# Retention and a cosine-gated MLP on one core: the first block by pairs of heads, and loads and weight differences in another order

## The chip, the cores and the metric

The kernel runs on one core of a Trainium2 chip. A core has five engines, each with a queue of its own: TensorE (PE; its weight loads are shown apart as PEld), VectorE (DVE), ScalarE (ACT), GpSimd (POOL) and SyncE (SP), which here only issues DMAs. All DMAs of a core run on the same 16 DMA engines. The metric is the time of one execution in microseconds (us) of device time, with all inputs in HBM at the start and the output in HBM at the end.

## The reference

```python
# q, k, v: [8 batches, 8 heads, 576 positions, 64], float32
scores = q @ k.transpose / sqrt(64)
gamma  = 1 - 2 ** (-5 - head)
Dmat   = gamma ** (i - j) for i >= j, else 0
attn   = (scores * Dmat) @ v
x      = attn, as [8 * 576 tokens, 8 * 64 = 512]
h      = x @ w_in          # [512, 2048]
out    = (h * cos(h)) @ w_out      # [2048, 512]
```

There is no softmax, so the retention can be computed block by block with a carried state, the running sum of k (transposed) times v.

## The kernel before, in words

**Retention.** The 4608 tokens are cut into 18 blocks `j` of 256. The decay is split: q is scaled by gamma to the power of its position (`gq`), k by gamma to the negative power (`gkp` for blocks 0 and 1, `gkc` for the rest), so that within a chunk the scores only need a mask of ones and zeros. The steps of a block are:

- `load(j)`: q, k and v from HBM by DMAs on SP. Blocks 0 and 1 put two neighbouring tokens into one partition (512 bytes in a run), and later blocks do so only for q.
- `scaled` (line 174): q or k times its decay, cast to bf16, one call for each of two token rows `y`. `prep(j)` issues the four calls of a block on GpSimd.
- `round_v` (line 185): v cast to bf16.
- `transpose_pe` (blocks 0 and 1, line 225) or `turned` (line 210): transposes on TensorE into a PSUM bank, which are then copied to `qkT` (lines 230 and 216).
- `scores` (lines 264 and 302): the matmuls of k and q by chunk, and the mask multiplication `masked` on VectorE, which writes `ret` (lines 282 and 311).
- `sums_of` (lines 352 and 335): the state matmuls of k and v. It returns `add`, which adds up the state `s_all` (lines 367 to 384), and that returns `rounded`, the copy to bf16 `sb` (line 394).
- `outputs`: `out_own` (line 420), `ret` times v; `out_carried` (line 447), the carried state times q; then the copy of PSUM `ov` to `xT` (lines 466, 853 and 499).

**MLP.** Two blocks make a window `n` of 512 tokens; there are nine. `mm1` (line 490) multiplies `w_in` by `xT` into PSUM `h`, four or two 128-column tiles at a time, ScalarE computes the cosine (line 503) and VectorE multiplies (line 506) into `gT`. The second product is plain in window 0 (line 991); from window 1 on it is done with seven instead of eight quarter products (`mm2_seven`, line 610), for which differences and sums of quarters of `w_out` (`w_sums`, line 529) and of `gT` (`g_sum`, line 549) are formed, mostly on VectorE. `w_sums` runs once, in window 0: (5, e0), (6, e0), (4, e0) and (7, e0), each for e0 = 0 and 4.

**Order.** The schedule is manual: each engine executes its instructions in the order in which the program issues them, and waits only for data and for buffers to come free. The opening (lines 760 to 871) is written out by hand. The queues around it are:

- SP: `load(0)`, `load(1)` with v behind k's landing, then `load_next` for blocks 2, 3 and 4. The first has a gate: its first DMA waits until the fourth `w_in` load has landed. That of block 3 waits for the third `w_out` load.
- GpSimd: position tables, `ident` and masks, the first `w_in` load, k of block 1, the other three `w_in` loads, half of v of block 1, `w_out` loads 0 and 4, load 8 (which waits for the landing of load 0, by `after`), k of block 2, `w_out` load 12, a half of q of block 2, then v of block 2 and `prep(3)`. Behind these stands `prep(4)`, which is issued in window 1. The weight loads convert float32 to bf16 on the way.
- `warm(n, tag)` puts n matmuls of zeros with 512 columns into a PSUM bank: fillers for TensorE.

In window 0 the matmuls of line 991 are issued in a loop with a counter `done` (0 to 63), and a list `todo` says which other step is issued at which count, lowest first: scaling, turning and scoring of blocks 2 and 3 and the weight differences. At equal count the order of the list holds. The results in PSUM (`o`, two parts in bank "m", one each in "n" and "st") are copied out by ScalarE and VectorE in turn (line 1001), and the first `mm1` of window 1 writes bank "m" again.

PSUM banks are named by tags: "a", "b" and "m" hold 4 KB per partition, "n" and "st" 2 KB. Each has one buffer, so a new tile in a bank waits until all readers of the old one are done.

## Time and profile before

| | |
|---|---|
| median of 3 runs | 296.82 us (296.63 to 296.84) |
| profiled execution | 296.85 us, its span 295.1 us |
| TensorE / VectorE / ScalarE / GpSimd busy | 284.5 / 215.2 / 170.5 / 143.4 us |
| first `h` matmul of window 0 | at 15.52 us |
| first `o` matmul of window 0 | at 31.69 us |
| first `h` matmul of window 1 | at 49.44 us |
| granted TensorE clock | 1.00 |

The rows of the time line read: start, duration, engine, source line, operation, output and inputs by the program's names, form, count; in brackets the idle time of the engine before it and what ended it. Rows of equal instructions close together are merged: the duration is then that of the whole row. Starts of instructions on one engine can lie closer together than their durations, since they overlap at the ends. Busy matmuls are modelled and overlap too. "SPq" and "POOL ... DMA_DIRECT2D" are the issues of DMAs, and "to landing" is the time from issue until the last of the data is there.

### The profile page before, as it was taken

What the parts mean: (1) busy time and instruction counts of PE and PEld (TensorE: products, weight loads), DVE (VectorE), ACT (ScalarE), POOL (GpSimd) and SP (SyncE); (2) the same over time, 40 slices, a digit from 0 to 9 for tenths busy, and PEclk for the clock granted to TensorE, in tenths of its full rate; (3) what the DMA queues carried; (4) which work ended last, traced back from release to release, by engine and by line L of the source; (5) the groups of instructions that cost most, each with busy time, mean ns of one, the idle gap of its engine ahead of it and who ended that gap; (6) DMA issues with size and microseconds to landing.
All of it is one profiled execution on the core that took longest, in us unless ns stands there. A gap on an engine that the chain in (4) does not pass through costs nothing.

```text
span 295.1 us, 10506 instructions
## 1 busy us (share of the span) xinstructions
PE 284.5 (96%) x4367; PEld 196.3 (67%) x4388; DVE 215.2 (73%) x300; ACT 170.5 (58%) x200; POOL 143.4 (49%) x163
## 2 busy tenths in 40 slices
PE   7899999999999999999999999999999999999994
PEld 2578545878864687468745884588458845884584
DVE  5756767758857887698769866986698669745943
ACT  3676317476558844767476737674768466535620
POOL 8621439970585995349434942495249014102400
PEclk9999999999999999999999999999999999999999
DMA  7999999999989857833873396429201130112013
GB/s 222 289 206 224 227 251 233 260 231 221 227 189 232 218 134 173 201 71 98 213 189 77 78 225 176 100 52 257 58 0 40 38 73 0 40 47 62 2 36 107
DMA packets 103981, 42.62 MB, mean 144 GB/s; under 512 B 68480, under 2 KB 103424, under 8 KB 103936
## 3 DMA queue, kind: packets, MB, share of 16 engines
q1 hardware_dynamic: 99184, 37.37, 51.8%
q0 software_dynamic: 4224, 4.19, 8.7%
q8 instruction: 36, 0.59, 0.9%
q10 hardware_dynamic: 528, 0.39, 0.4%
q14 instruction: 9, 0.07, 0.1%
HBM read 36.70 MB, written 9.44 MB: 156 GB/s over the span
## 4 chain that ended last, share of the span: by engine, by line
PE 83%; DVE 5%; ACT 3%; DMA 3%; POOL 2%; SPq 1%; issue 1%; ACTq 0%; DVEq 0%
PE h L490 41%; PE o L610 32%; PE ov L420 3%; PE tr L210 2%; POOL qks L174 2%; DMA fq<-in_q_dram 2%; PE ov L447 1%; PE sc L302 1%; DMA fk<-in_k_dram 1%; DVE gT L506 1%; PE st L335 1%; ACT cosh L503 1%; SPq L153 1%; DVE qks L174 1%; DVE ret L282 1%
## 5 line engine op out<-in xcount | busy, mean ns | idle before, releaser
L490 PE MATMUL h<-xT,w_in_sb 128*128 128x512 bf16 (+1 forms) x689 | 126.8, 340 | 1.3 <-DVE qkT L216 0.4
L506 DVE TENSOR_TENSOR gT<-h,cosh 128x1024 bf16<-128x1024 f32 x72 | 87.7, 1222 | 33.5 <-ACT cosh L503 33.1
L490 PEld LDWEIGHTS <-w_in_sb 128*128 128x128 bf16 x704 | 68.1, 98 | 55.2 <-issue 1.1
L503 ACT ACTIVATE cosh<-h,half_pi 128x1024 f32<-128x1024 f32 x72 | 79.9, 1115 | 40.5 <-PE h L490 40.5
L549 POOL TENSOR_TENSOR gs<-gT 128x512 bf16<-128x512 bf16 x28 | 35.8, 1277 | 100.4 <-DVE gT L506 100.4
L610 PEld LDWEIGHTS <-gs 128*128 128x128 bf16 x528 | 49.7, 98 | 5.9
L610 PEld LDWEIGHTS <-gT 128*128 128x128 bf16 x384 | 36.6, 98 | 6.1
L636 DVE TENSOR_TENSOR ot<-ot,o 128x512 f32<-128x512 f32 x35 | 23.2, 683 | 22.4 <-ACT ot L640 14.2
L174 POOL TENSOR_TENSOR qks<-fk,gkc 128x512 bf16<-128x512 f32 x32 | 37.1, 1178 | 2.8 <-DMA fk<-in_k_dram 2.8
L174 POOL TENSOR_TENSOR qks<-fq,gq 128x512 bf16<-128x512 f32 x31 | 34.7, 1137 | 7.5 <-DMA fq<-in_q_dram 7.5
L216 ACT COPY qkT<-tr 128x1024 bf16<-128x1024 bf16 x29 | 27.7, 1022 | 6.4 <-PE tr L210 6.4
L394 ACT CAST sb<-s_all 128x768 bf16<-128x768 f32 (+2 forms) x18 | 16.3, 904 | 25.6 <-DVE s_all L384 21.6
L610 PE MATMUL o<-w_out_sb,gs 128*128 128x256 bf16 (+1 forms) x264 | 30.6, 269 | 0.1
L610 PE MATMUL o<-w_out_sb,gT 128*128 128x256 bf16 x256 | 30.6, 273 | 0.0
L610 PE MATMUL o<-ws,gs 128*128 128x256 bf16 (+1 forms) x264 | 30.5, 269 | 0.0
L640 ACT COPY ot<-o 128x512 f32<-128x512 f32 x33 | 19.3, 584 | 16.0 <-PE o L610 16.0
L311 DVE TENSOR_TENSOR ret<-sc,mask_c 128x512 bf16<-128x512 f32 x32 | 20.7, 685 | 7.3 <-PE sc L302 7.3
L185 POOL CAST vb<-fv 128x512 bf16<-128x512 f32 x31 | 19.3, 646 | 4.8 <-DMA fv<-in_v_dram 4.8
L466 ACT CAST xT<-ov 128x1024 bf16<-128x1024 f32 x16 | 16.2, 1012 | 9.4 <-PE ov L447 9.2
L384 DVE TENSOR_TENSOR s_all<-st,s_all 128x256 f32<-128x256 f32 x49 | 20.7, 422 | 1.2
L549 DVE TENSOR_TENSOR gs<-gT 128x512 bf16<-128x512 bf16 (+1 forms) x25 | 16.7, 668 | 0.5
L610 PE MATMUL o<-ws,gT 128*128 128x256 bf16 x128 | 15.3, 273 | 0.0
(73 smaller groups left out, 207.0 us busy)
## 6 DMA issues: line engine op xcount, KB each, us to landing
out_dram<-ot SPq DMA_DIRECT2D x68, 128.0 KB, 2.6
fk<-in_k_dram SPq DMA_DIRECT2D x28, 256.0 KB, 4.9
fv<-in_v_dram SPq DMA_DIRECT2D x28, 256.0 KB, 4.8
fq<-in_q_dram SPq DMA_DIRECT2D x12, 512.0 KB, 5.1
w_in_sb<-in_moe_w_in_dram POOLq DMA_DIRECT2D x4, 512.0 KB, 8.0
w_out_sb<-in_moe_w_out_dram POOLq DMA_DIRECT2D x4, 512.0 KB, 8.3
fq<-in_q_dram SPq DMA_DIRECT2D x4, 384.0 KB, 5.1
fk<-in_k_dram SPq DMA_DIRECT2D x2, 512.0 KB, 4.9
```

What stands on the lines that cost most here:

```text
L174: return eng.tensor_tensor(out=dst.rearrange("p b a d -> p a b d"), in0=src.rearrange("p (a b) d -> p a b d", a=2), in1=by.rearrange("p (a ...
L185: runs[y](vb[:, y], f[:, :, y, :] if j < NP_B else f[:, y])
L216: evacs[r](tiles["qkT", j][:, :, :, :, r * HP : r * HP + HP], pss[r])
L311: nc.vector.tensor_tensor(out=ret[:, he].rearrange("p b y i -> p (b y) i"), in0=ps[he].rearrange("p b y i -> p (b y) i"), in1=mask_c.unsqu ...
L384: nc.vector.tensor_tensor(out=s32[:, u], in0=ps[c.half][:, c.y], in1=s32[:, u - 1] if u else tiles["run"], op=ALU.add,)
L490: nc.tensor.matmul(ps[:, j, :], lhsT=w_in_sb[:, dg, (et + j) * P : (et + j + 1) * P], rhs=xT[:, dg, c0 : c0 + w], start=(dg == 0), stop=(d ...
L503: nc.scalar.activation(cosh, ps, ACTF.Sin, bias=half_pi, scale=1.0)
L506: nc.vector.tensor_mul(gT[:, et : et + m, c0 : c0 + w], ps, cosh)
L549: i = eng.tensor_tensor(out=tiles["gs", n, x][:, e : e + step], in0=a[:, e : e + step], in1=b[:, e : e + step], op=op_,)
L610: nc.tensor.matmul(dst[i], lhsT=lhs[:, e, j * P : (j + 1) * P], rhs=rhs[:, e, c0:c1], start=(fresh and e == 0 and (i == 0 or len(parts) > 2)),
L636: return lambda: nc.vector.tensor_tensor(out=out_, in0=in0, in1=in1, op=ALU.add)
L640: held.append(lambda ps=tiles["all", x]: nc.scalar.copy(t, ps))
```

## The change

1. **Loads of block 0.** q and k of block 0 are loaded in two halves `g` of the heads (heads 0, 1, 4, 5 and then 2, 3, 6, 7), each by two DMAs, in the order k, q, k, q. Of the first halves one DMA each goes on ScalarE's queue, all others on SP. v follows as before.
2. **Block 0 by pairs of heads.** Scaling, transposes, copies, scores and masks are issued by halves: `scaled_heads`, `turned_heads`, `scores` with a range of head pairs. The copies of the transposes are all on ScalarE, and the masks come in two lots of 512 columns a head group instead of one of 1024. v is rounded half on GpSimd. The fillers are 8, 1, 1, 2 and 2 instead of 11, 2, 3, 2 and 2.
3. **Outputs of block 0 first.** `out_own(0)` now comes before the first transposes of block 1, and the copy to `xT` right behind `out_carried(0)` and ahead of the rest of block 1; q of block 1 is scaled, turned and copied row by row, one of the copies on ScalarE.
4. **Gates.** Block 2's loads wait for the third `w_in` load instead of the fourth, `w_out` load 8 no longer waits, and block 3's loads wait for the second `w_out` load instead of the third.
5. **Window 0's list.** Scores and state of block 2 are issued at 38 and 39 instead of 40 and 41; the weight differences (6, 0), (4, 0), (7, 0) come behind them instead of at 34 to 36; q of block 3 is scaled on VectorE at 40, its k on GpSimd; then the differences (6, 4), (4, 4), (7, 4) at 41 to 43 instead of 51 to 53.

Branches that no call used are removed from `scores` and `prep`.

```diff
+    def load_heads(name, g):
+        src = {"q": q, "k": k}[name]
+        if ("f" + name, 0) not in tiles:
+            tiles["f" + name, 0] = ld.tile([P, H, 2, D], F32, tag="f" + name, name=f"f{name}")
+        f = tiles["f" + name, 0]
+        for he in range(2):
+            h0 = he * HG + 2 * g
+            (nc.scalar if he and not g else nc.sync).dma_start(
+                f[:, h0 : h0 + 2].rearrange("p h r d -> p h (r d)"),
+                src[0, h0 : h0 + 2, :BK, :].rearrange("h (p r) d -> p h (r d)", r=2),
+            )
+
+    def scaled_heads(eng, name, g):
...
+        for y in range(2):
+            eng.tensor_tensor(
+                out=dst[:, y],
+                in0=f[:, y],
+                in1=by[:, y, 2 * g : 2 * g + 2].unsqueeze(3).to_broadcast([P, 2, 2, D]),
+                op=ALU.mult,
+            )
+
+    def turned_heads(name, g, bank, evac=nc.scalar.copy):
...
+        ps = psum.tile([P, 2, 2, P], BF16, tag=bank, name="tr")
+        for y in range(2):
+            for u in range(2):
+                nc.tensor.transpose(
+                    ps[:, y, u, :],
+                    tiles["qks", 0][:, m, y, 2 * g + u].rearrange("s a d -> s (a d)"),
+                    ident,
+                )
+        evac(tiles["qkT", 0][:, m, :, 2 * g : 2 * g + 2], ps)
+
-    def prep(j):
-        for name in "kq" if j < NP_B else "qk":
+    def prep(j, eng_q=nc.gpsimd):
+        for name in "qk":
             for y in range(2):
-                scaled(nc.gpsimd, j, name, y)
+                scaled(eng_q if name == "q" else nc.gpsimd, j, name, y)
...
-    def scores(j, banks):
+    def scores(j, banks, g0=0, g1=HG):
...
-    load(0, "kqv")
+    for g in range(2):
+        for name in "kq":
+            load_heads(name, g)
+    load(0, "v")
     k1 = load(1, "k")
...
-    warm(11, "n")
+    warm(8, "b")
...
-    scaled(nc.vector, 0, "k", 0)
-    scaled(nc.vector, 0, "k", 1)
-    transpose_pe(0, "k", "n", act, (0,))
-    transpose_pe(0, "k", "st", act, (1,))
-    scaled(nc.vector, 0, "q", 0)
-    scaled(nc.vector, 0, "q", 1)
-    transpose_pe(0, "q", "a", act, (0,))
-    transpose_pe(0, "q", "b", vec, (1,))
+    scaled_heads(nc.vector, "k", 0)
+    turned_heads("k", 0, "n")
+    scaled_heads(nc.vector, "q", 0)
+    warm(1, "b")
+    turned_heads("q", 0, "st")
+    scaled_heads(nc.vector, "k", 1)
+    warm(1, "b")
+    turned_heads("k", 1, "m")
+    scaled_heads(nc.vector, "q", 1)
+    masks = scores(0, "ab", 0, 2)
+    turned_heads("q", 1, "n")
+    for masked in masks:
+        masked()
     w_dma = [load_w_in(0)]
-    round_v(0, (act, act))
     warm(2, "m")
-    for masked in scores(0, "ab"):
+    masks = scores(0, "ab", 2, HG)
+    round_v(0, (nc.gpsimd.tensor_copy, act))
+    for masked in masks:
         masked()
+    warm(2, "m")
     sums_of(0, "st")()()
     scaled(nc.gpsimd, 1, "k", 0)
-    warm(3, "m")
-    transpose_pe(1, "k", "n", act, (0,))
     scaled(nc.gpsimd, 1, "k", 1)
     w_dma += [load_w_in(e) for e in (512, 1024, 1536)]
-    load_next(names="kqv", gate=w_dma[3])
+    load_next(names="kqv", gate=w_dma[2])
     ps0 = psum.tile([P, DG, BK], F32, tag="m", name="ov")
     out_own(0, ps0)
-    scaled(nc.vector, 1, "q", 0)
-    scaled(nc.vector, 1, "q", 1)
-    transpose_pe(1, "k", "st", vec, (1,))
+    transpose_pe(1, "k", "n", act, (0,))
     out_carried(0, ps0)
     act(x_of(0), ps0)
+    scaled(nc.vector, 1, "q", 0)
+    transpose_pe(1, "k", "st", vec, (1,))
+    transpose_pe(1, "q", "a", act, (0,))
+    scaled(nc.vector, 1, "q", 1)
+    transpose_pe(1, "q", "b", vec, (1,))
     nc.scalar.activation(sine, half_pi, ACTF.Sin, bias=0.0, scale=1.0)
     round_v(1, (act, nc.gpsimd.tensor_copy))
-    warm(2, "n")
-    transpose_pe(1, "q", "a", vec, (0,))
-    transpose_pe(1, "q", "b", vec, (1,))
-    warm(2, "n")
     for masked in scores(1, "ab"):
         masked()
     w_dma += [load_w_out(e) for e in (0, 4)]
     w_dma.append(load_w_out(8))
-    after(w_dma[-1], w_dma[4])
     for y in range(2):
         scaled(nc.gpsimd, 2, "k", y)
     w_dma.append(load_w_out(12))
     scaled(nc.gpsimd, 2, "q", 0)
-    load_next(names="kqv", gate=w_dma[6])
+    load_next(names="kqv", gate=w_dma[5])
     load_next()
...
-                (40, lambda: adds.append(states_and_scores(2, "a", "b"))),
-                (41, lambda: adds.pop()()()),
-                (42, lambda: prep(3)),
+                (38, lambda: adds.append(states_and_scores(2, "a", "b"))),
+                (39, lambda: adds.pop()()()),
+                (40, lambda: prep(3, nc.vector)),
...
-                    (2, 5, 0), (8, 5, 4), (34, 6, 0), (35, 4, 0), (36, 7, 0),
-                    (51, 6, 4), (52, 4, 4), (53, 7, 4),
+                    (2, 5, 0), (8, 5, 4), (39.2, 6, 0), (39.4, 4, 0), (39.6, 7, 0),
+                    (41, 6, 4), (42, 4, 4), (43, 7, 4),
```

## The prediction

> **What bounds the kernel now.** I read the page first, then the time line of single engines over the first 52 us, then the landing of single loads. All times are us from the start of the span of the one profiled execution, which took 296.85 us (295.1 of span and 1.75 around it); the median of the runs shown is 296.82. The page:
>
> ```profile
> PE 284.5 (96%) x4367; PEld 196.3 (67%) x4388; DVE 215.2 (73%) x300; ACT 170.5 (58%) x200; POOL 143.4 (49%) x163
> ...
> DMA  7999999999989857833873396429201130112013
> ```
>
> TensorE is busy 96% of the span, so only its waits can be won: those ahead of the first matmul on `w_in` (15.52) and those up to some 52 us, the only stretch that the change touches. The DMA row is full from the second slice to the eleventh. TensorE from 15:
>
> ```profile
> 15.52 1.92 PE L490 MATMUL h<-xT,w_in_sb 128*128 128x256 bf16 x16
> ...
> 19.00 1.05 PE L490 MATMUL h<-xT,w_in_sb 128*128 128x256 bf16 x8
> ...
> 20.33 1.92 PE L490 MATMUL h<-xT,w_in_sb 128*128 128x256 bf16 x16
> ```
>
> After eight of the last row's matmuls (0.11 each), at 21.21, begins the third group of `w_in` columns, 1024 to 1535. The load of these columns, the third of the four on line 742:
>
> ```profile
> L742 POOL DMA_DIRECT2D w_in_sb<-in_moe_w_in_dram x1: 747/747/747, 12.2 to 12.2; - x1
> ...
> DMA to landing us min/median/max: 8.9/8.9/8.9
> ```
>
> It lands at 21.1, 0.1 before its use. The one before it lands at 18.6 (11.4 and 7.2), 0.4 before its use at 19.00. An earlier start of TensorE soon meets a weight still on its way, and the DMA engines are full ahead of it (time by stretches, last two columns their mean share and GB/s):
>
> ```profile
> 0.00:4.00 4.00, 2.75 (x7) 1.01 (x8) 1.56 (x15) 1.91 (x4) 2.73 (x21) 1.00 0.40 117
> 4.00:8.00 4.00, 3.46 (x22) 1.47 (x21) 2.79 (x4) 1.47 (x4) 3.80 (x8) 1.00 1.15 346
> 8.00:12.00 4.00, 3.04 (x86) 1.90 (x88) 3.01 (x4) 2.98 (x6) 2.58 (x3) 1.00 1.20 286
> ```
>
> The second place is the end of window 0, VectorE and then GpSimd:
>
> ```profile
> 44.71 2.60 DVE L529 TENSOR_TENSOR ws<-w_out_sb,ws 128x1024 bf16<-128x1024 bf16 x2
> 47.24 1.53 DVE L529 TENSOR_TENSOR w_out_sb<-w_out_sb 128x1024 bf16<-128x1024 bf16 x1
> 48.69 0.69 DVE L1001 COPY ot<-o 128x512 f32<-128x512 f32 x1
> ```
>
> ```profile
> 43.28 2.04 POOL L174 TENSOR_TENSOR qks<-fq,gq 128x512 bf16<-128x512 f32 x2 [2.80 <-DMA fq<-in_q_dram]
> 45.28 2.94 POOL L174 TENSOR_TENSOR qks<-fk,gkc 128x512 bf16<-128x512 f32 x2
> 48.18 2.48 POOL L174 TENSOR_TENSOR qks<-fq,gq 128x512 bf16<-128x512 f32 x2
> ```
>
> ```profile
> 47.40 0.52 PE L210 MATMUL tr<-ident,qks 64*128 64x64 bf16 x24
> 48.27 0.29 PE L210 MATMUL tr<-ident,qks 64*128 64x64 bf16 x8 [0.35 <-POOL qks L174]
> 48.50 1.04 PE L991 MATMUL o<-w_out_sb,gT 128*128 128x512 bf16 x4
> 49.44 1.47 PE L490 MATMUL h<-xT,w_in_sb 128*128 128x256 bf16 x12
> ```
>
> Two things are to be seen. TensorE loses 0.5 at 48.27, where block 3's transposes wait for GpSimd. And the first `h` of window 1 starts at 49.44, 0.06 after VectorE's copy of `o` (48.69 and 0.69) has emptied PSUM bank "m", which this `h` takes. So VectorE's queue is a limit there too. In it the weight differences (line 529) took 1.15, 1.42 and 1.53 beside GpSimd's scalings, against 0.68 with GpSimd idle (34.18), and GpSimd's k took 1.49 each against 1.04: starts lie 1.45 apart when they alternate, 0.605 when VectorE runs alone.
>
> **The change, part by part.** First the loads of block 0. Two loads of 512 KB become eight of 128 KB, six on SP, two on ACT. Bytes and the DMA engines are the same, and the data of k was all there at 4.67 (0.80 and 3.9); half of it I put at 3.9, since at 346 GB/s the other 256 KB take 0.75. On SP the six issues at 0.43 to 0.57 take 3 us where two took 1.0, and v of block 0, then k, q and v of block 1, stand behind them; the engines are full meanwhile, so this is hidden, as long as an issue of 128 KB (0.38 us of transfer at 346 GB/s) does not cost more than it carries. If it did, block 0's four pairs would be issue-bound: bound 0 to +1.0. I take 0. On ACT two issues go ahead of the table load (0.80 and 1.28), which then ends near 3.1, ahead of the first exponential at 3.28: hidden.
>
> The chain of block 0: eight scalings of 256 columns (0.34 each by 0.60 for 512, 0.42 beside GpSimd's masks) from 4.0, when both k and the decay (3.28 and 0.23, then `kpos` until 3.87 on VectorE) are there, until 7.3 instead of 7.6. Transposes and copies follow by pairs; scores of the first two head pairs near 7.1 to 7.7, masks 4 x 0.62 in two lots, the second until 10.2 to 10.7 instead of 11.78. State matmuls 9.8 to 10.8, outputs 10.8 to 11.8 instead of 12.7. Rounding v moves half to GpSimd, free from 7.97 until k of block 1 at 9.4: hidden.
>
> Block 1's transposes now stand behind. VectorE's order is q row 0, copy of k row 1, q row 1, copy of q row 1. The copy of k waits for TensorE (12.8), so q row 1 comes at 13.3 to 13.9, its transposes at 14.0, its copy until 14.8, the scores at 14.85, the first `h` at 15.45. What the first block gained, the order of the second gives back: -0.07. Were it 0.3 earlier, the weight landing at 21.1 would take all but 0.1 of it. GpSimd's queue up to the `w_in` loads has only the half round of v put in, inside its wait; those loads land as before. Sum of the first part: -0.1 to +0.3, and I take 0.
>
> Loads of blocks 2 and 3: SP's gate goes from the fourth `w_in` load (23.6) to the third (21.1), and the third `w_out` load no longer waits for the first (GpSimd stood 8.35 us for that, in front of k of block 2). The order on the engines changes, their work does not; fq of block 2 comes earlier than 35.9 and the sums need nothing of it before 37.8. The fourth `w_out` load still follows k of block 2 on GpSimd. If k lands only at 32, behind the third `w_out` load, the fourth is issued near 34 instead of 32.03; landing took 7.1 then (39.1), so it is there by 41, and its first use is at 43.6, hidden by the `o` matmuls; past that, each us late would cost one. Nothing else waits on these in 31 to 42: 0.
>
> End of window 0, where X is the first part's shift. Scores of block 2 are issued two matmuls of 0.213 earlier, at 40.67; masks (0.61 x 2, by 1.28 for the two at 42.27) from 41.4, state adds until 43.86 instead of 44.71, so the carried outputs no longer wait for the state (0.28 won, 45.72 in the trace). VectorE is idle for 1.2 before it, having nothing else in front. After it come three weight differences, q of block 3 (two, new on VectorE), and three differences: eight operations at 0.605, until 48.70 alone, then the copy of `o` until 49.35. That is the same 49.4 as now: what VectorE is spared of GpSimd (2.4) it pays with q (1.2) and idleness (1.2). TensorE would be ready for `h` at 48.65, and waits.
>
> So the question is what GpSimd does from 43.86 to 48.70. Its k of block 3 should be over by 43.9 (data near 40.8). Next in its queue are q of block 4, whose second load was issued at 43.85 and landed 4.1 later, at 47.95. The bytes ahead of it are unchanged, so I keep 48.0, with 0.5 either way. At 48.05 seven of the eight are over or running; GpSimd takes the turn, the last difference comes 0.85 later (1.45 less 0.605), the copy ends at 50.25, `h` starts at 50.3: +0.86. Block 3's scores, which now wait 0.16 for a copy on ACT (51.03), then don't. Sum +0.7.
>
> That price is 0.85 a turn by the rows. [...]
>
> **The rivals.**
> No turn: q of block 4 lands after 48.1, or GpSimd comes too late. Then `h` starts at 49.40 and the ACT wait is gone: -0.2, 296.6. For it: 0.1 of margin only. Against: nothing delays that load.
> Two or more turns: block 3's gate is earlier and the DMA share fell to 0.59 in 40 to 41 and 0.84 in 44 to 45; closed, these gaps bring q of block 4 up to 0.6 earlier, to 47.4, where two differences are left: +0.7 and 0.85, 298.4.
> Faster, the other side: two queues fill the engines sooner. The first 4 us moved 117 GB/s, and if the full rate came 0.85 earlier, k of block 1 and all weights would land that much earlier, and block 1's chain with them; with the first `h` at 14.9 and no turn lost the sum is -0.5 and -0.2, 296.1. It decides once the third `w_in` load lands before 20.6.
> The array's clock: the fillers fall from 20 to 14, and seven that stood between 10 and 14.6 become two before 9.9. In the trace fillers started 0.43 apart until 5.9 and 0.22 apart at 7.9, with the granted clock at 1.00 throughout. If TensorE met `h` at the slow pace, 16 matmuls would cost 0.11 more each, +1.75, 298.6, or with issue-bound loads +1.0. [...]
>
> **How the numbers follow.** 0.2% is 0.6 us, about what a measurement of this kernel can tell from no change. One turn, my forecast: 0.38, of which 0.05 inside the 0.6. No turn: 0.20. Faster, with ways that I don't see: 0.20. Two or more turns: 0.14. Clock or issue-bound loads: 0.08. So faster 0.20, same 0.25, slower 0.55. The time is 296.82 and 0.7: 297.5. The range reaches down past the faster case by its own margin, 295.9, and up to two turns with the first part at +0.3 and half a turn more, 299.2. The forecast case alone spans 297.3 to 297.9.
>
> **What would show it.** Right: the third `w_in` load lands near 21.1 and TensorE's third group begins with it; the first `h` of window 1 starts on the heels of VectorE's copy of `o` at 50 or later, with a TensorE gap above 1 ahead of it; the last of the eight VectorE operations takes over 1.1 beside GpSimd's q of block 4; block 3's transposes no longer wait. Wrong: an `h` there before 49, eight operations of 0.68 throughout, or weights that land before 20.6.

## The result: slower, by twelve microseconds, and not by the same amount each time

The changed kernel took 309.23 us (median of 4, 304.81 to 311.14) against 296.83 for the kernel before: a ratio of 1.0324, 95% interval 1.0231 to 1.0417. Forecast were 297.5 and, as the range, 295.9 to 299.2. In a later group of runs the same kernel took 299.08, 306.55, 307.99 and 309.36. The ratios below leave out executions of over 1.5% above the quickest of their kernel, so for kernels that vary the whole spread of times is given too.

Two profiled executions of the changed kernel, one of 310.42 us and one of 299.08, are read beside each other. Times are from the start of the span. The page of the long one, with the lines that answer to those shown of before, and the granted clock:

```profile
PE 290.7 (94%) x4382; PEld 198.5 (64%) x4382; DVE 217.7 (71%) x306; ACT 171.5 (56%) x201; POOL 142.5 (46%) x162
...
PEclk9958999879999999999999999999999999999999
DMA  7999999997933894782488157906600140022013
```

TensorE is busy 6.2 us longer for the same work (290.7 against 284.5). Of the 40 slices of the clock, of 7.7 us each, the third is at 5 (half), the fourth and the eighth at 8 and the ninth at 7; before, all were whole. The DMA row is full from the second slice to the ninth, then thin in the twelfth and thirteenth. In the rows of the changed kernel the same steps have other line numbers: the scaling is L214 (174 before), rounding v L225 (185), `mm1` L520 (490), the weight differences L559 (529), the second product L1027 (991), the copy of `o` L1037 (1001).

| | before | changed, 310.42 | changed, 299.08 |
|---|---|---|---|
| q of block 1: scaling on VectorE can start | 10.71 (landed) | 16.50 | 11.80 |
| third `w_in` load lands | 21.10 | 22.91 | 21.81 |
| first `h` of window 0 | 15.52 | 20.40 | 15.57 |
| first `o` of window 0 | 31.69 | 38.64 | 32.35 |
| fourth `w_out` load lands | 39.09 | 45.05 | 44.69 |
| list of eight VectorE operations begins | | 50.90 | 44.97 |
| first `h` of window 1 | 49.44 | 60.38 | 51.49 |
| span | 295.1 | 308.6 | 297.2 |

The chain of work of the long execution, in order of time (start, duration, what), tells the course in a few lines:

```profile
5.19 11.29 DMA fq<-in_q_dram
16.50 0.69 DVE qks L214
...
20.47 3.53 PE h L520 x16
...
27.34 11.46 PE h L520 x104
...
52.91 2.90 DVE qks L214 x2
55.81 1.46 DVE ws L559
...
59.72 0.61 DVE ot L1037
...
60.38 2.72 PE h L520 x12
```

The load of q of block 1 takes 11.29 from issue to landing (before, 6.0). With it the first `h` moves by 4.88. Its 16 matmuls take 3.53 in this chain where they took 1.85, and by the first `o` the delay is 6.95. Then VectorE's list takes 8.74 (50.90 to 59.64), where the same eight operations alone take 5.06 (shown further down): 3.68 more. 4.88, 2.07 and 3.68 are 10.6 of the 10.9 at the first `h` of window 1; behind that come 2.6 more, to the 13.5 by which the span is longer, with the clock at half again. By stretches (start and end, length, then the busy time of PE, PEld, DVE, ACT and POOL with counts, the granted clock, and the DMA engines' share and GB/s):

```profile
12.00:16.00 4.00, 0.98 (x16) 0.54 (x16) 0.00 (x0) 1.60 (x3) 3.14 (x4) 0.86 1.18 249
16.00:20.00 4.00, 1.82 (x32) 1.32 (x36) 2.05 (x4) 2.07 (x4) 1.96 (x3) 0.50 1.24 214
20.00:24.00 4.00, 4.00 (x38) 2.56 (x31) 2.35 (x2) 0.51 (x1) 0.82 (x2) 0.50 1.24 206
...
60.00:64.00 4.00, 3.62 (x47) 2.40 (x46) 1.21 (x3) 0.00 (x0) 4.00 (x5) 0.50 0.97 234
```

So there are three mechanisms (a late load, a halved clock and the turns of VectorE and GpSimd), and in the execution of 299.08 the second is missing and the first is down to 1.1. The experiments ask what sets each off, and what the parts of the change cost alone. In their diffs `-` is the kernel named and `+` the experiment. The kernel before, run beside them, had medians of 297.1 to 297.7.

### The profile page after: what moved, and what is told of

It is laid out like the page before. It is cut to its first block, busy times and chain, and to the rows that moved or that the text cites. A ratio compares the mean times of both kernels' runs of the same rounds, so it can differ in the third digit from the quotient of the medians.

```text
span 308.6 us, 10530 instructions
## 1 busy us (share of the span) xinstructions
PE 290.7 (94%) x4382; PEld 198.5 (64%) x4382; DVE 217.7 (71%) x306; ACT 171.5 (56%) x201; POOL 142.5 (46%) x162
## 4 chain that ended last, share of the span: by engine, by line
PE 84%; DVE 7%; DMA 5%; ACT 3%; issue 1%; SPq 0%; DVEq 0%; ACTq 0%
PE h L520 41%; PE o L640 30%; DMA fq<-in_q_dram 4%; PE o L1027 3%; PE ov L450 2%; PE tr L250 2%; PE sc L332 1%; DVE qks L214 1%; DVE ws L559 1%; PE ov L477 1%; PE st L365 1%; DMA fk<-in_k_dram 1%; DVE ret L341 1%; DVE s_all L414 1%; DVE gT L536 1%; ACT cosh L533 1%
## 5 line engine op out<-in xcount | busy, mean ns | idle before, releaser
L520 PE MATMUL h<-xT,w_in_sb 128*128 128x512 bf16 (+1 forms) x704 | 132.0, 349 | 3.7 <-DVE ot L1037 3.0
L520 PEld LDWEIGHTS <-w_in_sb 128*128 128x128 bf16 x704 | 70.1, 101 | 60.5 <-issue 4.8
L214 POOL TENSOR_TENSOR qks<-fk,gkc 128x512 bf16<-128x512 f32 x32 | 37.2, 1180 | 18.8 <-DMA fk<-in_k_dram 18.8
L214 POOL TENSOR_TENSOR qks<-fq,gq 128x512 bf16<-128x512 f32 x29 | 32.6, 1143 | 5.9 <-DMA fq<-in_q_dram 5.8
L225 POOL CAST vb<-fv 128x512 bf16<-128x512 f32 x32 | 20.8, 675 | 4.8 <-DMA fv<-in_v_dram 4.8
## 6 DMA issues: line engine op xcount, KB each, us to landing
w_out_sb<-in_moe_w_out_dram POOLq DMA_DIRECT2D x4, 512.0 KB, 10.9
```

The costliest lines, as they stand in the source:

```text
L214: return eng.tensor_tensor(out=dst.rearrange("p b a d -> p a b d"), in0=src.rearrange("p (a b) d -> p a b d", a=2), in1=by.rearrange("p (a ...
L225: runs[y](vb[:, y], f[:, :, y, :] if j < NP_B else f[:, y])
L520: nc.tensor.matmul(ps[:, j, :], lhsT=w_in_sb[:, dg, (et + j) * P : (et + j + 1) * P], rhs=xT[:, dg, c0 : c0 + w], start=(dg == 0), stop=(d ...
```

## Experiments on the first part

**The small loads alone.** The kernel before, with the loads of block 0 of the change and nothing else:

```diff
-    load(0, "kqv")
+    for g in range(2):
+        for name in "kq":
+            load_heads(name, g)
+    load(0, "v")
```

> The kernel before with the eight loads of 128 KB (six on SP, two on ACT) in place of the two of 512 KB, everything else as before. Theory: the loads alone make q of block 1 land at 14 to 16.5 and the first h of window 0 at 18 to 20.4, with a half clock behind: +3 to +7, 300 to 304. Rival: the loads alone cost only their issue, 1.0 to 1.5: 297.8 to 298.3.

Measured: 302.46 (299.86 to 306.70), ratio 1.0113 (1.0018 to 1.0209). In the profiled execution (299.86) VectorE waits for q of block 1 until 15.27, and the first `h` comes at 18.18. The theory holds: these loads alone delay block 1, and by more than their issue.

**Why q is late.** In the changed kernel SP issues 128 KB every 0.5 (0.44 to 0.49 each), which is 262 GB/s; from 4 to 8 the engines moved 280 GB/s where they had moved 346 (least from 4 to 5, 215). That the small loads cause this is shown by the run with whole loads below (347 again); that it is their issue, and not something else about them, is argued from these figures. So v of block 0 lands at 9.22 instead of 7.68 and k of block 1 at 10.71 instead of 9.24. GpSimd meanwhile issues its `w_in` load at 6.54, earlier than before (7.02). The DMA queues (q1 is SP's, q0 GpSimd's; packets, MB, share of the time of 16 engines) in the long execution from 9 to 11 and from 11 to 13:

```profile
q1 hardware_dynamic: 866, 0.44, 77.4%
q0 software_dynamic: 103, 0.11, 34.3%
...
q0 software_dynamic: 271, 0.28, 82.0%
q1 hardware_dynamic: 263, 0.13, 33.0%
```

and in the execution of 299.08 from 9 to 11:

```profile
q1 hardware_dynamic: 1160, 0.58, 98.5%
q0 software_dynamic: 35, 0.04, 14.9%
```

There SP's queue has moved 0.58 MB when `w_in` has hardly begun (35 packets), and q is as good as through (ready at 11.80). The margin is small: in two runs below with the same loads, the old end and the first fillers alone, SP moved 0.63 and 0.60 MB in this stretch beside 8 and 33 packets of `w_in`, and q was ready only at 14.90 and 14.89. By 11 SP had moved 2.33 MB in all in the execution of 299.08, 2.29 and 2.23 in the runs with the fillers and the old end, and 2.16 in the long one: what is left of q then, even where it is under 0.1 MB, is held up beside `w_in`. In the long execution SP has moved 0.44 and `w_in` has 103 packets in; from 11 to 13 the two queues have as many packets (271 and 263) but not as many bytes: 0.28 MB and 0.13, some 1.03 KB a packet of `w_in` against 0.49 on SP's queue. By time of the engines it is 82 to 33, and the last of q comes at 16.48, after `w_in` (16.32). The `w_in` load was issued at 6.54 and 6.55 in the two executions; why its packets began earlier in the one, no run shows.

**Whole loads.** The changed kernel with the two loads of 512 KB:

```diff
-    for g in range(2):
-        for name in "kq":
-            load_heads(name, g)
-    load(0, "v")
+    load(0, "kqv")
```

> The changed kernel with q and k of block 0 loaded by the two DMAs of 512 KB on SP as before, everything else changed. Theory: the eight small loads are issue-bound and let the first w_in load overtake q of block 1; with whole loads q of block 1 lands near 10.7 again, the first h comes near 15.5, there is no idle time above 1 us ahead of it and no half clock; the end of window 0 meets one or two turns: 297 to 299. Rival: block 0 by pairs, with block 1 behind it, is what delays; the first h stays near 20 and the time at 307 to 310.

Measured: 301.63 (298.83 to 306.35), ratio 1.0081 (1.0030 to 1.0132). q of block 1 lands at 10.87, as before. That part of the theory holds, but the first `h` comes at 17.22, not 15.5: neither theory. The rest of that delay must lie in the order, which was then run alone.

**The order alone.** The kernel before with block 0 by pairs, its outputs first and fewer fillers; loads, gates and the end of window 0 as before. From the changed kernel (the gates and the list put back are shown with the runs on them below):

```diff
-    for g in range(2):
-        for name in "kq":
-            load_heads(name, g)
-    load(0, "v")
+    load(0, "kqv")
...
-    load_next(names="kqv", gate=w_dma[2])
+    load_next(names="kqv", gate=w_dma[3])
...
-                (40, lambda: prep(3, nc.vector)),
+                (42, lambda: prep(3)),
```

> The kernel before with the order of the first part alone: block 0 by pairs of heads, its outputs ahead of block 1's keys and queries, fewer fillers; the two whole loads of 512 KB, the gates and the end of window 0 as before. The forecast's step says 0: first h at 15.5, 296.8. The theory from the runs so far: the order itself delays, since block 1's copies and scalings now stand behind block 0's outputs and the clock falls to half between 8 and 12 with fewer fillers; first h near 17.2, 298.5 to 299.5.

Measured: 299.00 (298.25 to 304.63), ratio 1.0063 (1.0030 to 1.0096); first `h` at 16.86. The order costs 1.3 at the first `h`. The clock by single microseconds in that run:

```profile
4.00:5.00 1.00, 0.44 (x2) 0.00 (x0) 0.09 (x1) 0.17 (x1) 0.95 (x5) 1.00 1.15 345
...
6.00:7.00 1.00, 0.49 (x5) 0.11 (x2) 0.65 (x2) 0.58 (x1) 1.00 (x2) 1.00 1.15 348
...
8.00:9.00 1.00, 1.00 (x21) 0.63 (x20) 0.87 (x3) 0.67 (x2) 0.59 (x1) 0.50 1.15 348
```

With TensorE busy 0.44 to 0.49 of each microsecond from 4 to 7, the clock is at half from 7.3 to 10.7 (0.66 and 0.64 in the microseconds at the ends). No idle time there is longer than 0.95. The next run fills these two idle times:

```diff
-    warm(8, "b")
+    warm(10, "b")
...
     scaled_heads(nc.vector, "q", 0)
-    warm(1, "b")
+    warm(2, "b")
```

> The pairs alone (whole loads, gates and end of window 0 as before) with three fillers more in the two idle times that stand ahead of the half clock there: 10 instead of 8 at the start, 2 instead of 1 behind the first k pair. Theory: with the clock whole between 7 and 11 the second scores and masks of block 0 come 0.6 to 0.9 earlier, the first h at 16.0 to 16.3 instead of 16.86, and the runs scatter less: 297.8 to 298.5. Rival: ScalarE's copies, not TensorE's clock, set that chain; the first h stays at 16.7 to 17 and the time near 299.

Measured: 298.07 (six of eight 297.97 to 299.22, two 301.64 and 302.77), ratio 1.0055 (1.0022 to 1.0088). The clock stays at 1.00, the first `h` comes at 16.54: 0.3 of the 1.3 was the clock. The other 1.0 is the order: TensorE waits 0.89 and 0.61 for VectorE's scaling and copy of q row 1, which stand behind the copy of k. With k of block 0 in halves (3.5 instead of 4.8) block 0 is a microsecond earlier, and the changed kernel's good execution has its first `h` at 15.57 after all.

**`w_in` behind v.**

```diff
-    load(0, "v")
+    v0 = load(0, "v")
...
     w_dma = [load_w_in(0)]
+    after(w_dma[0], v0)
```

> The changed kernel with its first w_in load issued only once v of block 0 has landed (about 9.2, instead of 6.5). Theory: the w_in load shares the engines with q of block 1 and holds it up; behind v it does not, q of block 1 lands near 12, its scaling starts there, TensorE's idle time of 3.9 ahead of its transposes falls under 1.5, the clock stays whole, and the first h comes at 16.5 to 17.5, with w_in landing near 15.5: 303 to 305, the end of window 0 still with its turns. Rival: q of block 1 is late by its own issue alone; it lands after 15 whatever w_in does, and the time stays at 307 to 311.

Measured: 302.11; ten executions, five from 298.78 to 300.39 and five from 303.82 to 312.17, with the mean clock at 0.999 to 1.000 in the first five and 0.965 to 0.980 in the others; ratio 1.0073 (1.0042 to 1.0104). In the profiled one (300.13) all steps of the theory are there: q scaled from 12.27, `w_in` landed at 15.53, the longest idle time ahead of the first `h` 0.89, and that `h` at 16.67. The executions above 303.8 were not explained by it. Two runs tried a wider margin.

```diff
+    after(w_dma[0], k1)
```

> The changed kernel with its first w_in load issued only once k of block 1 has landed (10.2 to 10.7), some 1.2 later than behind v. Theory: behind v the first packets of w_in (11.7) still meet the last of q of block 1 (11.5 to 12.2), and the executions of 304 to 312 there are those that q lost; behind k the margin is over 1, every execution keeps q near 12, and the scatter of 13 between executions shrinks to 3 or less: 299 to 302, first h near 17.3. Rival: the scatter comes from something other than this meeting, the clock above all, and executions of 304 and more remain.

Measured: 306.78 (304.57 to 308.03), ratio 1.0303 (1.0240 to 1.0367). q landed at 11.91 and the executions lie within 3.5, but on the high side: GpSimd, waiting until 10.70 for that load, rounds its half of v only behind it, and TensorE stands 1.89 at 10.47. The clock is at half from 13.1 to 23.3 and the first `h` at 19.27. The edit had put a new wait in place of the old. So, v first:

```diff
-    w_dma = [load_w_in(0)]
     warm(2, "m")
     masks = scores(0, "ab", 2, HG)
     round_v(0, (nc.gpsimd.tensor_copy, act))
+    w_dma = [load_w_in(0)]
+    after(w_dma[0], k1)
```

> As the run with w_in behind k of block 1, but GpSimd rounds its half of v of block 0 ahead of that load instead of behind it. There q of block 1 landed at 11.9, yet GpSimd's wait held v, TensorE stood 1.89 at 10.5 and the clock fell to half from 13 to 21. Theory: with v first that idle time is under 1, the clock stays whole, w_in lands near 17, the first h comes at 17.0 to 17.5, and the executions lie within 3 of one another: 299 to 302. Rival: the clock falls anyway (first h at 19 or later) or executions of 304 and more remain, so that neither the meeting of the loads nor that wait is the cause: 304 to 308.

Measured: 303.63 (300.57 to 304.71), ratio 1.0161 (1.0072 to 1.0250). q landed at 12.14, `w_in` at 17.31, and the executions lie within 4.1. But the idle times add up (1.35, then 0.56 and 0.61), VectorE's scaling takes 2.37 beside GpSimd's k of block 1, and the clock goes again:

```profile
12.00:14.00 2.00, 0.63 (x12) 0.37 (x12) 1.83 (x1) 0.59 (x3) 2.00 (x3) 1.00 0.93 248
14.00:16.00 2.00, 1.25 (x12) 0.80 (x12) 1.49 (x3) 1.93 (x4) 2.00 (x3) 0.74 1.23 211
16.00:18.00 2.00, 1.39 (x36) 1.03 (x35) 0.56 (x2) 1.62 (x3) 2.00 (x4) 0.50 1.24 203
```

The first `h` comes at 17.77 with 16 matmuls in 3.60. With q in time no execution was above 308.03 in the one run and 304.71 in the other (four each); the half clock was not gone, so the rival has that half. The meeting itself is shown as the cause of the late q by all profiles together: in the five with `w_in` held back (these three and the two of the repairs below) VectorE could begin with q of block 1 at 11.93 to 12.28, in the seven with these loads as changed six times at 14.89 to 16.50 and once at 11.80. What sends a single execution with `w_in` behind v above 303.8 stays open.

## Experiments on the clock

**Fillers in both idle times of the long execution**, 3.9 and 3.0:

```diff
+    warm(16, "b")
     transpose_pe(1, "q", "a", act, (0,))
...
                     stores.append((u * P, ot))
+            warm(12, "b")
             continue
```

> The changed kernel with fillers on zeros in TensorE's two long idle times: 16 ahead of the transposes of q of block 1, 12 ahead of the first h of window 1. Theory: the halved clock behind each idle time costs by itself 2.1 and 2.4; with TensorE kept busy the first 16 h take 1.9 instead of 3.6 and the h of window 1 run at 0.11 instead of 0.21 each, while both idle times stay: 304.5 to 306. Rival: what follows is bound by late loads, so that a whole clock only turns into waits: 308 to 310.

Measured: 303.01 (301.81 to 303.51), ratio 1.0178 (1.0127 to 1.0229), with the clock at 0.998 to 1.000 in all four. q of block 1 is as late as ever (15.72), yet the kernel is 6.2 and 4.3 quicker than the two medians of the changed kernel:

```profile
13.25 3.40 PE L275 MATMUL idle<-zeros 128*128 128x512 bf16 x15
...
19.00 1.92 PE L520 MATMUL h<-xT,w_in_sb 128*128 128x256 bf16 x16
```

16 `h` matmuls in 1.92 again. It is more than the theory gave: the list on VectorE, which now begins at 47.43 instead of 50.90, is nearly over when q of block 4 lands (51.77), and takes 5.06. The 12 fillers ahead of window 1 were too many; they run past the copy of `o`, and `h` waits for them until 54.62.

**The first fillers alone**, none ahead of window 1:

```diff
+    warm(16, "b")
     transpose_pe(1, "q", "a", act, (0,))
```

> The changed kernel with the 16 fillers ahead of the transposes of q of block 1 only (none ahead of window 1). Theory: the half clock of the first h costs 1.7 to 2.1, and it also pushes VectorE's list into GpSimd's scaling of block 4; with the first clock whole the list is over before most of the turns and the second idle time falls to 1.5 or less, so most of what both sets of fillers won comes from the first: 303 to 305. Rival: the two idle times cost separately; with the second unfilled the idle time of 3 and its half clock stay: 306 to 308.

Measured: 303.27 (301.38 to 304.00), ratio 1.0196 (1.0156 to 1.0236). As good as with both, so it is the first half clock that brings on most of the rest. The idle time ahead of window 1 is 1.88, above the 1.5 of the theory, and the clock from 52 to 56 is still 0.69.

## Experiments on the gates

**The gates alone**, in the kernel before:

```diff
-    load_next(names="kqv", gate=w_dma[3])
+    load_next(names="kqv", gate=w_dma[2])
...
-    after(w_dma[-1], w_dma[4])
...
-    load_next(names="kqv", gate=w_dma[6])
+    load_next(names="kqv", gate=w_dma[5])
```

> The kernel before with the gates of the change alone (blocks 2 and 3 behind the third w_in load and the second w_out load, the third w_out load not held behind the first). Theory, the step of the forecast: 0, 296.8. Rival: the earlier third w_out load holds up the loads of blocks 2 to 4 by 2 to 4, and VectorE's list at the end of window 0 comes later or meets GpSimd: +1 to +3.

Measured: 300.76 (299.58 to 301.47), ratio 1.0103 (1.0058 to 1.0149). The rival holds, by its first half. GpSimd:

```profile
32.88 1.04 POOL L174 TENSOR_TENSOR qks<-fk,gkc 128x512 bf16<-128x512 f32 x1 [13.71 <-DMA fk<-in_k_dram]
34.73 1.27 POOL L174 TENSOR_TENSOR qks<-fk,gkc 128x512 bf16<-128x512 f32 x1 [0.81 <-DMA fk<-in_k_dram]
35.95 0.81 POOL L748 DMA_DIRECT2D w_out_sb<-in_moe_w_out_dram  x1
```

and TensorE:

```profile
44.66 1.46 PE L990 MATMUL o<-w_out_sb,gT 128*128 128x512 bf16 x6 [0.73 <-DMA w_out_sb<-in_moe_w_out_dram]
...
49.25 0.29 PE L210 MATMUL tr<-ident,qks 64*128 64x64 bf16 x8 [0.65 <-POOL qks L174]
...
51.24 0.29 PE L210 MATMUL tr<-ident,qks 64*128 64x64 bf16 x8 [0.71 <-POOL qks L174]
...
52.34 0.93 PE L490 MATMUL h<-xT,w_in_sb 128*128 128x256 bf16 x7
```

The third `w_out` load, no longer held, is issued at 18.40 instead of 26.53, and its 512 KB pass in front of block 2. k of block 2 is all there at 34.66 instead of 30.70, so GpSimd issues the fourth `w_out` load, which stands behind k, at 35.95 instead of 32.03; it lands at 44.61 instead of 39.09, where TensorE waits 0.73. q of block 3, behind it, lands near 47 instead of 43.21, and its transposes wait 0.65, 0.71 and 0.71 for GpSimd. The first `h` of window 1 comes at 52.34: 2.9 late.

**The changed kernel with the old gates:**

```diff
-    load_next(names="kqv", gate=w_dma[2])
+    load_next(names="kqv", gate=w_dma[3])
...
+    after(w_dma[-1], w_dma[4])
...
-    load_next(names="kqv", gate=w_dma[5])
+    load_next(names="kqv", gate=w_dma[6])
```

> The changed kernel with the gates of blocks 2 and 3 and of the third w_out load put back. Theory: alone the gates cost some 3 because the fourth w_out load and q of block 3 come late; in the changed kernel TensorE is late itself by 5 to 7 and they are mostly hidden: 307 to 310. Rival: the costs add, 305 to 306.5.

Measured: 300.19, 300.27, 308.68 and 309.72 (ratio 1.0098, 1.0065 to 1.0131, by the two low ones). Neither theory: the kernel varies as the changed one does, and the gates don't decide which. Little can be read from it on the gates; its low times lie 1 above the 299.08 of the changed kernel's own.

## Experiments on the end of window 0

**The end alone**, in the kernel before:

```diff
-                (40, lambda: adds.append(states_and_scores(2, "a", "b"))),
-                (41, lambda: adds.pop()()()),
-                (42, lambda: prep(3)),
+                (38, lambda: adds.append(states_and_scores(2, "a", "b"))),
+                (39, lambda: adds.pop()()()),
+                (40, lambda: prep(3, nc.vector)),
...
-                    (2, 5, 0), (8, 5, 4), (34, 6, 0), (35, 4, 0), (36, 7, 0),
-                    (51, 6, 4), (52, 4, 4), (53, 7, 4),
+                    (2, 5, 0), (8, 5, 4), (39.2, 6, 0), (39.4, 4, 0), (39.6, 7, 0),
+                    (41, 6, 4), (42, 4, 4), (43, 7, 4),
```

> The kernel before with the end of window 0 of the change alone (scores, states, differences in the new order, q of block 3 on VectorE). Theory, the step of the forecast: q of block 4 lands near 48 as before, GpSimd takes one turn of 0.85, first h of window 1 at 50.3, +0.7: 297.5. Rival: the new order meets several turns whatever the loads do, as in the changed kernel: +3.9, with a halved clock behind the idle time +2.4: 300.7 to 303.

Measured: 297.51 (296.76 to 299.06), ratio 0.9998 (0.9967 to 1.0030). VectorE's list and GpSimd beside it:

```profile
44.10 1.41 DVE L529 TENSOR_TENSOR ws<-w_out_sb,ws 128x1024 bf16<-128x1024 bf16 x2
...
46.03 1.29 DVE L174 TENSOR_TENSOR qks<-fq,gq 128x512 bf16<-128x512 f32 x2
...
49.16 1.28 DVE L1001 COPY ot<-o 128x512 f32<-128x512 f32 x2
...
49.14 2.04 POOL L174 TENSOR_TENSOR qks<-fq,gq 128x512 bf16<-128x512 f32 x2 [6.15 <-DMA fq<-in_q_dram]
```

Eight operations from 44.10 to 49.16, at 0.63 each. q of block 4 landed at 48.98, and GpSimd began when the list ended: no turn, and the first `h` of window 1 at 49.90. This is the forecast's list in its own conditions. In the changed kernel's long execution GpSimd could begin with block 4 at 52.32, 3.2 later than there, but the list began 6.8 later:

```profile
50.90 1.41 DVE L559 TENSOR_TENSOR ws<-w_out_sb,ws 128x1024 bf16<-128x1024 bf16 x2
...
52.83 2.98 DVE L214 TENSOR_TENSOR qks<-fq,gq 128x512 bf16<-128x512 f32 x2
55.73 2.97 DVE L559 TENSOR_TENSOR ws<-w_out_sb,ws 128x1024 bf16<-128x1024 bf16 x2
...
59.64 1.28 DVE L1037 COPY ot<-o 128x512 f32<-128x512 f32 x2
...
52.32 2.94 POOL L214 TENSOR_TENSOR qks<-fq,gq 128x512 bf16<-128x512 f32 x2 [5.64 <-DMA fq<-in_q_dram]
55.23 2.93 POOL L214 TENSOR_TENSOR qks<-fk,gkc 128x512 bf16<-128x512 f32 x2
58.11 2.09 POOL L225 CAST vb<-fv 128x512 bf16<-128x512 f32 x2
```

From 52.32 each engine's operation takes turns with one of the other's: 1.45 to 1.5 each, instead of 0.6 and 1.04. Five of VectorE's eight are caught, the last by a cast of v (58.11), which takes 1.05 instead of 0.61.

**GpSimd's block 4 held back** until VectorE has copied `o` (in the changed kernel):

```diff
-                scaled(eng_q if name == "q" else nc.gpsimd, j, name, y)
+                i = scaled(eng_q if name == "q" else nc.gpsimd, j, name, y)
+                if j == 4 and name == "q" and not y:
+                    after(i, held_by[0])
...
-                    (act, vec)[u % 2](ot[:, 0], pss[u])
+                    ot_copy = (act, vec)[u % 2](ot[:, 0], pss[u])
+                    if u == 1:
+                        held_by.append(ot_copy)
```

> The changed kernel with GpSimd's scalings of block 4 held until VectorE has copied o at the end of window 0. Theory: without the turns VectorE's list takes 0.6 to 0.7 an operation, TensorE's idle time of 3.0 ahead of the first h of window 1 falls to under 1.5 and the clock stays whole: 302 to 305. Rival: the list is late because its data (q of block 3, landed at 47.1) and its masks are late; without turns the idle time stays above 2.5, and block 4, now late, delays window 1: 308 to 312.

Measured: 302.26 (298.23 to 304.02), ratio 1.0113 (1.0022 to 1.0203). In the profiled execution (304.02) the first `h` of window 0 comes at 20.07, as late as in the long execution, but the list takes 5.07 (50.12 to 55.19), none of it over 0.71 an operation, TensorE stands 1.03 instead of 3.01, and `h` starts at 55.92 instead of 60.38 (line numbers two higher than in the changed kernel):

```profile
53.26 1.41 DVE L561 TENSOR_TENSOR ws<-w_out_sb,ws 128x1024 bf16<-128x1024 bf16 x2
...
55.92 1.47 PE L522 MATMUL h<-xT,w_in_sb 128*128 128x256 bf16 x12 [1.03 <-DVE ot L1039]
```

The clock, at half from 9.78 to 23.44 in this execution, stays at 1.00 from there on. That the turns cost 3.7 is shown by this run, and so is that without them the second half clock is gone. From that `h` to the end it takes 246.2 where the long one takes 248.2; so that half clock costs about 2, as far as two executions can tell.

**The old end in the changed kernel**, the reverse of the diff of the end alone:

```diff
-                (40, lambda: prep(3, nc.vector)),
+                (42, lambda: prep(3)),
...
-                    (41, 6, 4), (42, 4, 4), (43, 7, 4),
+                    (51, 6, 4), (52, 4, 4), (53, 7, 4),
```

> The changed kernel with the end of window 0 put back as before (order of block 2's scores, states and weight differences; q of block 3 on GpSimd). Theory: the first part alone costs the start of the first h (20.4 against 15.5) and half a clock behind it, +4.9 and +2.1 = about 7; what the end adds by its order (3.9, and 2.4 of half clock behind its idle time) is gone: 303 to 304. Rival: the late loads of blocks 3 and 4, which come from the first part, stretch any order of the end: 307 to 309.

Measured: 302.80 (301.76 to 305.52), ratio 1.0168 (1.0081 to 1.0254). The theory, but for a tenth or two; in the profiled execution (301.86) the first `h` is at 18.80, 3.3 late, and its 16 matmuls are at half clock. So the new end, which costs nothing alone, costs 4.5 to 6.4 by the medians behind a late first part.

**An attempt at a quicker one**: the end alone, with its last three differences behind the copy of `o`.

```diff
-                    (41, 6, 4), (42, 4, 4), (43, 7, 4),
+                    (56, 6, 4), (56.1, 4, 4), (56.2, 7, 4),
```

> The kernel before with the end of window 0 of the change and its last three weight differences put behind VectorE's copy of o. Theory: VectorE's list is what the first h of window 1 waits for (1.03 of idle time in the run with the end alone); with the list 1.9 shorter h follows the last o at 48.9 instead of 49.4 (before) and 49.9 (end alone): 296.3, faster than both. Rival: the three differences then delay block 3's masks beside GpSimd's scalings, and what is won at h is lost at block 3: 296.8 to 297.5.

Measured: 302.31 (300.46 to 303.06), ratio 1.0159 (1.0131 to 1.0187). `h` does start earlier than with the end alone (49.47), but the three differences now stand between VectorE's two copies of `o`, beside GpSimd's block 4, and the scores of block 3 wait for the bank of the second copy:

```profile
49.33 2.99 DVE L529 TENSOR_TENSOR ws<-w_out_sb,ws 128x1024 bf16<-128x1024 bf16 x2
52.24 1.52 DVE L529 TENSOR_TENSOR w_out_sb<-w_out_sb 128x1024 bf16<-128x1024 bf16 x1
53.69 0.68 DVE L1001 COPY ot<-o 128x512 f32<-128x512 f32 x1
...
54.42 0.44 PE L302 MATMUL sc<-qkT 64*64 64x64 bf16 x31 [3.34 <-DVE ot L1001]
```

Three differences take 4.4 instead of 1.9, and TensorE stands 3.34. The rival named the place (block 3) but not the price.

## All repairs together

The changed kernel with `w_in` behind v, the old gates, four fillers ahead of the transposes of q of block 1 and four ahead of window 1:

```diff
+    after(w_dma[0], v0)
...
-    load_next(names="kqv", gate=w_dma[2])
+    load_next(names="kqv", gate=w_dma[3])
...
+    warm(4, "b")
     transpose_pe(1, "q", "a", act, (0,))
...
+    after(w_dma[-1], w_dma[4])
...
-    load_next(names="kqv", gate=w_dma[5])
+    load_next(names="kqv", gate=w_dma[6])
...
+            warm(4, "b")
             continue
```

> The changed kernel with three repairs: first w_in load behind v of block 0, the gates put back, four fillers ahead of the transposes of q of block 1 and four ahead of the first h of window 1. Theory: late q of block 1, late loads and the half clock are all of the loss but some 1 to 1.5 of the order: first h near 16.7, clock whole, 297.5 to 299.5 without scatter. Rival: the loss has another part, and it stays above 301.

Measured: 299.73 (299.22 to 301.07), ratio 1.0096 (1.0064 to 1.0128). A little above the theory's range; the spread is down from 10 to 1.9. The first `h` is at 17.47: the clock was at 0.57 from 12 to 16, and the four fillers ran in it. With fillers in the idle times of 0.8 at 6.1 and 10.2 in place of the four ahead of the transposes:

```diff
     scaled_heads(nc.vector, "q", 0)
-    warm(1, "b")
+    warm(2, "b")
...
-    warm(2, "m")
+    warm(4, "m")
     sums_of(0, "st")()()
...
-    warm(4, "b")
     transpose_pe(1, "q", "a", act, (0,))
```

> The changed kernel with the first w_in load behind v of block 0, the gates put back, four fillers ahead of window 1, and three fillers more in the idle times of 0.8 in the first 11 us instead of four ahead of the transposes of q of block 1. Theory: with no half clock between 12 and 16 the first h comes at 16.3 to 16.8, 298 to 299. Rival: the half clock there costs nothing since q of block 1 is waited for anyway; 299.5 to 300 as with the four fillers.

Measured: 300.07 (299.03 to 302.20), ratio 1.0122 (1.0082 to 1.0162). The clock is whole and the first `h` comes at 16.53, as the theory said, but the time is no better; most of the 0.94 won there is given back before window 1, whose first `h` comes at 51.49 against 51.74. And the changed kernel once more, with no edit:

> The changed kernel itself, once more, for a measure of its scatter beside the kernels of this group. 304 to 312; the runs with two half clocks 308 to 312, with one 304 to 306.

Measured: 307.27 (299.08 to 309.36). Its lowest time was not expected at all. No version beat the kernel before; the end alone equals it.

## Why the prediction was wrong, step by step

**The small loads, taken as 0, is the step that failed most.** Its condition ("as long as an issue of 128 KB ... does not cost more than it carries") was not met: 0.49 for an issue, against 0.38 of transfer. The text bounded that at +1.0 and charged it to block 0's pairs. But block 0 was in time (masks over at 10.70, forecast 10.2 to 10.7); the delay fell on what SP issues behind them: in the long execution v of block 0 and k of block 1, each 1.5 late, and q of block 1, 5.8 late. Block 1's chain was then worked out from 12.8 on as if q were there, as in the trace of before, although the same working had put six issues in front of it. Where q was there, in the execution of 299.08, that chain came out: first `h` at 15.57, forecast 15.45.

**"Those loads land as before"** failed with it. The working asked of GpSimd's `w_in` loads only when they are issued, not what they meet. In the long execution the first met q of block 1 (16.48 instead of 10.71). Even where it hardly did, the other three were issued behind a k of block 1 that was 1.0 late, and landed 0.6 to 0.7 late; from this comes the first `o` at 32.35.

**The clock** was given 0.08, together with the issue-bound loads; no row of before showed how likely it was. The price given, 1.75 for 16 matmuls, was right (3.60 less 1.92 is 1.68), but the half clock lasted beyond these 16 and came a second time. Nor did it take a long idle time: the order alone has half clock from 7.3 to 10.7, behind idle times of 0.95 and 0.51. What decides was not shown; what was measured is told at the end.

**The gates, taken as 0**, cost 2.9 alone. The text saw the right chain ("If k lands only at 32 ... the fourth is issued near 34 ... past that, each us late would cost one") and mis-sized it: k was there at 34.66, the load issued at 35.95 and there at 44.61, past the 43.6 of its use. What it did not follow is q of block 3, on the same engines behind it, 3.9 late. All this is from the gates alone; what they cost in the changed kernel was not measured.

**The end of window 0** was right in its mechanism, but not in the event forecast. VectorE's copy of `o` sets the first `h` of window 1, eight operations and the copy alone end near 49.4 (49.8 in the run with the end alone), and a turn, put at 0.85, cost 0.72 in the execution of 299.08, 0.74 as the mean of five in the long one, and 0.85 with the first fillers alone (list 5.91 for 5.06, its last difference 1.53 beside q of block 4, the very turn of the forecast).

But q of block 4, put at 48.0 with 0.5 either way, landed at 48.98 with the end alone, so that turn fell away there; why it landed later no run shows. The list began 0.24 later than worked out and took 0.22 more, and `h` came at 49.90 without a turn. That the median of the end alone, 297.51, is the time forecast is luck.

The mistake was to carry the first part's shift as a number to be added, X, with one turn fixed. Between the end alone and the long execution GpSimd's q of block 4 shifted by 3.2, since it comes by DMAs, and the list, which comes by TensorE, by 6.8; so the difference decides the number of turns: none in the end alone, one in the execution of 299.08, five in the long one. In that of 299.08 the sum works out: 49.90 (end alone), 0.87 for the later beginning of the list (44.97 for 44.10) and 0.72 for a turn (5.78 for 5.06) make 51.49, which is what the profile shows. That turn is with k of block 3, which the forecast had over by 43.9 and which GpSimd begins at 45.26, not with q of block 4 (50.80):

```profile
44.97 2.13 DVE L559 TENSOR_TENSOR ws<-w_out_sb,ws 128x1024 bf16<-128x1024 bf16 x2
```

Of the rivals, "two or more turns", "clock" and "issue-bound loads" all came true, and together; each had been given a time of its own as if the others were absent. Even so the best execution of the changed kernel, 299.08, lies just inside the range; its course is near the forecast's, with three terms to correct (loads of `w_in` 0.7, the list alone 0.46, the later gates), but its one turn is another than the one forecast, so part of that is luck. The other seven, of which one was profiled, had mean clocks of 0.966 to 0.982: a different course, which no case had.

## What to carry to other kernels

When loads are split or moved, follow every queue that stands behind them on the issuing engine, and ask of each load on another queue whether it now begins before an older one has ended: from that moment an urgent load and a patient one share the engines, and here the one with the larger packets got more (0.28 MB against 0.13 from 11 to 13 of the long execution). Where the margin between two such loads is as small as here, with q of block 1 ready at 11.80 in one execution and at 16.50 in another, one profile is not enough to judge by. And costs of different parts don't add where a late engine meets work that is timed by DMAs (here the list came 6.8 later and GpSimd's q of block 4 3.2, and there were five turns instead of none): shift the one against the other before counting turns.

## What was not expected of the hardware

**The clock did not go by the length of an idle time.** It fell to half with idle times of 0.95 and 0.51 (the order alone) and with one of 1.46 (the small loads alone), but stayed whole through 3.34 in the run with the late differences, where TensorE does nothing in this stretch and the clock is 1.00 there and behind:

```profile
52.00:54.00 2.00, 0.00 (x0) 0.00 (x0) 2.00 (x3) 0.00 (x0) 2.00 (x2) 1.00 1.05 294
```

In the long execution the microseconds in which the clock changes are these:

```profile
14.00:15.00 1.00, 0.00 (x0) 0.00 (x0) 0.00 (x0) 0.00 (x0) 1.00 (x2) 0.92 1.24 304
25.00:26.00 1.00, 0.90 (x39) 0.58 (x34) 0.76 (x2) 0.18 (x2) 0.00 (x0) 0.96 1.25 206
59.00:60.00 1.00, 0.00 (x0) 0.00 (x0) 1.00 (x2) 0.00 (x0) 1.00 (x2) 0.61 0.63 140
66.00:67.00 1.00, 1.00 (x11) 0.88 (x10) 1.00 (x1) 0.00 (x0) 1.00 (x2) 0.98 1.03 234
```

A mean of 0.92 with steps between 1 and 0.5 puts the fall at 14.84; the others come to 25.08, 59.22 and 66.04. The distances are 10.24, 34.14 and 6.82, which is 3, 10 and 2 times 3.41. The shortest distance in any of these profiles is as long itself: with whole loads the clock is at half from 8.30 to 11.70. Four more profiles (whole loads, the old gates and the two with `w_in` behind k of block 1) have four steps each, and all their distances are whole multiples of 3.41, to within 0.04; the run with the old gates, for one, falls at 9.82, rises at 23.46, falls at 57.60 and rises at 64.42, which is 4, 10 and 2 times 3.41. In the 3.41 ahead of both falls of the long execution TensorE was partly busy: ahead of 14.84 it has matmuls until 13.35 and 1.31 of busy time, ahead of 59.22 it has 1.49. That an idle time of 1 to 3 us halves the clock or not by where it falls between two such steps is the author's estimate from these distances; no run shows it. That this is also behind the executions above 303.8 with `w_in` behind v was only argued, from their mean clocks (0.965 to 0.980).

**Two loads that meet.** The same program, with the issues on SP at the same times to 0.01 until 4.4 us, had q of block 1 ready at 11.80 in one execution and at 16.50 in another.
